# Attention with a learned position bias and a dense block: bias rows read from a gapped table, a new hand-written order, and one store per half of the last block

## The chip, the cores and the metric

The kernel runs on one core of one Trainium2 chip. The metric is the device time of one execution in microseconds; three executions of the kernel before took 640.33, 636.6 and 635.3 us, the median is 636.6. A profile is one more execution with the hardware profiler on.

The engines are named as in the profile: PE is the matrix engine (PEld its weight loads), DVE the vector engine, ACT the scalar engine, POOL the general-purpose engine (GpSimd), SP the engine whose queue issues almost all transfers here. DVE and ACT read and write both memories of the core, PSUM (where PE writes its sums) and SBUF; POOL reads and writes SBUF.

## What is computed

```
scores = q @ k^T / sqrt(64)              # 4 batches, 8 heads, 576 positions, 64 wide
x      = log1p(|i - j|) / log1p(max(i, 1))
bias   = relu(x * w1 + b1) @ w2          # hidden size 32, one column of w2 per head
attn   = softmax(scores + bias)          # with 1e-9 in the denominator
out    = attn @ v                        # heads joined: 2304 tokens of 512
h      = relu(out @ w_in)                # 512 -> 2048
result = (h * h) @ w_out                 # 2048 -> 512
```

Inputs and result are in 32 bit, the weights of the dense block arrive as 64-bit numbers. Products are made in 16 bit from a high and a low part of each operand, three matmuls for one, so everything that PE reads is split first.

## The kernel before

**Stages.** The 2304 tokens are ten blocks of 128 to 256 rows (two batches, five stretches of positions; the blocks of 64 positions take two batches into one tile, the others are 256 rows). For each of 80 pairs of block and head there are: scores on PE (qk, into one PSUM tile sc), one softmax step per batch on DVE that combines scores and bias and finds the extreme (L656, 144 in all), the exponential on ACT (L669), a conversion into high and low parts on ACT and POOL (L710, L712), a transpose (by PE for the first heads, by a DMA later), and the product with v (pv). When a block's eight heads are done it is scaled (norm) and transposed, and the dense block runs over its 16 hidden tiles in eight steps: 24 matmuls (g1, L837), a square (ACT L849, DVE L851, a cast, POOL L857), and the second product (g2, L872). The last block of 64 positions has its output halved in columns and is stored by `store` (L882 to 898).

**Before the steady state.** Two things are built in the first 240 us beside the attention. First the weights: each of 32 tiles of w_in and w_out is loaded as 64-bit numbers (`w_dma`), turned into a 32-bit number by three DVE instructions (L362 and L364 into PSUM, L369 into SBUF), and split by ACT and POOL (L278, L394). Second the bias: 36 groups of 16 positions, 4 rows of a small table each (`hgen`, tiles hg), multiplied by w2 on PE (`bias_mm`, L542), scaled by ACT or DVE (`bias_out`) and written to DRAM (biasd), from where each softmax step reads its bias tile (bt). The four groups of the first block are computed as max(table x w + c, ...) (L471, or ACT's L469). The 32 other groups use a table that was multiplied by -w1 once (ACT, L508, in place, so it must wait until the first four groups have read it) and take the minimum of it and one number per partition and row (DVE L477, 88 instructions, or ACT L473 with a relu, 40 instructions). They read L columns, 304 to 576, in one plain run.

**The order.** Nothing is scheduled by a compiler here. PROGRAM is a long text of some 2,550 words; each word names a step (hg:4.0 is half of the bias rows of the fifth group, ws:9 one piece of the ninth weight tile, sa a softmax step, bo a piece of the bias output, ou a store), and each occurrence lets that step issue its next instructions. Every engine then runs its own instructions strictly in that order and waits, through semaphores, for what an instruction needs. Transfers go through SP's queue in that order as well. A late instruction therefore holds up all that stands behind it on its engine.

**Names that the change touches.** tab_t holds the table (LW = 576 columns) and the scales; h2 is the buffer for two bias rows of S = 576 columns each; PATS and HID choose for each group how many of its four rows ACT computes (only the first three patterns are in use); hcst holds constants, its fourth column -w1; sm_t holds w1, b1 and w2.

Of the kernel before, what the change touches and what calls it, by code (L numbers as in the profile page):

```python
# [8 lines left out]
F32 = mybir.dt.float32  # L9
# [16 lines left out]
LW = 576  # L26
# [4 lines left out]
PATS = ["DDDD", "ADDD", "AADD", "DDDP", "DDPP", "ADDP", "ADPP", "AADP", "AAPP", "DPPP"]  # L31
# [170 lines left out]
def tile_attention_moe(  # L202
# [56 lines left out]
    sel = const.tile([128, 32], F32, name="sel")  # L259
    rows_s = const.tile([128, 36], F32, name="rows_s")  # L260
    nb1 = const.tile([128, 1], F32, name="nb1")
    hcst = const.tile([128, 4], F32, name="hcst")

    eps = const.tile([128, 2], F32, name="eps")
    esc = const.tile([128, 1], F32, name="esc")
# [752 lines left out]
```

## Time and profile before

| | us |
|---|---|
| median of three executions | 636.6 (635.3 to 640.33) |
| the profiled execution, its device time | 637.86 |
| its span from the first to the last instruction | 636.1 |
| PE busy | 597.7 (94%) |
| DVE busy | 428.1 (67%) |
| POOL busy | 385.4 (61%) |
| ACT busy | 366.5 (58%) |

A view of windows gives, for stretches of the span, how long each engine was busy in it; a group of instructions gives how many there are, their busy time together (overlaps counted once) and the mean length of one. Instructions of one engine overlap a little at their ends, so a group's busy time is a bit less than count times mean. A timeline row is an instruction, or a run of equal ones, with its start and length.

### The profile page before, as it was taken

The page shows a single profiled execution, that of the slowest core. Times are in us where ns is not written, and L with a number is a line of the kernel's source. Part 1 is how long each engine was busy: PE and PEld are TensorE (multiplying, and loading weights), DVE is VectorE, ACT ScalarE, POOL GpSimd, SP SyncE. Part 2 cuts the span into 40 slices and gives each one's busy share as a digit, 9 for nine tenths or more (in the row PEclk, how much of TensorE's full clock was granted, in tenths as well). Part 3 has the DMA queues.
Part 4 walks back from the last instruction along what each step waited for, and adds up shares of the span by engine and source line. Part 5 has one row for each costly group of instructions (what it writes and reads, how often), then busy time and mean ns, then how long its engine had stood idle before and what let it go on. Part 6 is the DMA issues. An engine that isn't in the chain of part 4 may idle for free.

```text
span 636.1 us, 15958 instructions
## 1 busy us (share of the span) xinstructions
PE 597.7 (94%) x6296; PEld 402.7 (63%) x6296; DVE 428.1 (67%) x840; ACT 366.5 (58%) x779; POOL 385.4 (61%) x389
## 2 busy tenths in 40 slices
PE   5658998899999999999999999999999999999997
PEld 2124576475767467667657865767676686577576
DVE  7988999899669796787974663566456463613321
ACT  5559997687777465645567455746636574214020
POOL 5766499989767435866866647555665555523221
PEclk9669999899999999999999999999999999999999
DMA  8999987778979969799789969559955787623000
GB/s 291 325 285 284 286 237 253 244 188 203 191 183 185 220 159 170 184 226 221 177 164 219 165 131 186 139 115 196 186 136 122 158 169 144 140 34 72 18 34 18
DMA packets 204426, 112.19 MB, mean 176 GB/s; under 512 B 166848, under 2 KB 179392, under 8 KB 204352
## 3 DMA queue, kind: packets, MB, share of 16 engines
q1 hardware_dynamic: 204272, 111.12, 75.2%
q8 instruction: 49, 0.80, 0.5%
q14 instruction: 25, 0.20, 0.1%
q10 hardware_dynamic: 80, 0.07, 0.0%
HBM read 55.44 MB, written 15.61 MB: 112 GB/s over the span
## 4 chain that ended last, share of the span: by engine, by line
PE 51%; DMA 5%; DVE 5%; POOL 4%; issue 3%; ACT 2%; SPq 1%; POOLq 0%; DVEq 0%; ACTq 0%
PE hp L837 20%; PE o L872 19%; PE pv L757 5%; PE sc L637 5%; DMA at<-a 3%; DMA xt<-xh 2%; POOL a L712 2%; PE bp L542 1%; DVE s L656 1%; POOL g L857 1%; DVE g L280 1%; ACT s L669 1%; DMA stg<-vd 1%; DVE r L851 1%; ACT a L276 1%
## 5 line engine op out<-in xcount | busy, mean ns | idle before, releaser
L837 PE MATMUL hp<-xt,winH 128*128 128x256 f16 (+1 forms) x1280 | 193.3, 262 | 2.0 <-DVE r L851 1.1
L872 PE MATMUL o<-woutH,g 128*128 128x512 f16 (+1 forms) x608 | 186.4, 369 | 2.2 <-POOL g L857 1.6
L837 PE MATMUL hp<-xt,winL 128*128 128x256 f16 (+1 forms) x640 | 161.7, 262 | 0.0
L857 POOL TENSOR_TENSOR g<-r,g 128x512 f16<-128x512 f32 (+1 forms) x80 | 88.4, 1108 | 88.3 <-DVE g L280 81.5
L872 PEld LDWEIGHTS <-g 128*128 128x128 f16 x912 | 84.3, 98 | 90.5 <-issue 4.5
L712 POOL TENSOR_TENSOR a<-s,a 128x1024 f16<-128x1024 f32 (+1 forms) x64 | 133.1, 2079 | 0.0
L837 PEld LDWEIGHTS <-winH 128*128 128x128 f16 x1280 | 117.8, 98 | 20.6 <-DVE r L851 1.2
L656 DVE CUSTOM_DVE_ANT_0 s<-sc,bt 128x576 f32<-128x576 f32 x144 | 104.6, 749 | 35.7 <-PE sc L637 15.2
L851 DVE TENSOR_TENSOR r<-hp,r 128x512 f32<-128x512 f32 (+1 forms) x80 | 50.7, 634 | 105.6 <-ACT r L849 105.2
L872 PE MATMUL o<-woutL,g 128*128 128x512 f16 (+1 forms) x304 | 112.1, 369 | 0.0
L669 ACT ACTIVATE s<-s,nm 128x576 f32<-128x576 f32 x120 | 92.9, 774 | 6.6 <-ACT nm L667 0.4
L710 POOL TENSOR_TENSOR a<-s,a 128x128 f16<-128x128 f32 (+1 forms) x64 | 30.3, 473 | 105.6 <-ACT a L276 73.7
L849 ACT ACTIVATE r<-hp 128x512 f32<-128x512 f32 (+1 forms) x80 | 43.7, 546 | 85.4 <-PE hp L837 75.2
L757 PE MATMUL pv<-v,at 128*128 128x64 f16 (+5 forms) x2112 | 87.8, 203 | 1.9 <-ACT at L276 1.2
L667 ACT ACTIVATE nm<-mx,esc 128x1 f32<-128x1 f32 x120 | 34.4, 287 | 84.2 <-DVE mx L656 84.0
L276 ACT ACTIVATE a<-s 128x1152 f16<-128x1152 f32 (+1 forms) x64 | 70.3, 1098 | 14.6 <-DMA at<-a 13.5
L837 PEld LDWEIGHTS <-winL 128*128 128x128 f16 x640 | 62.6, 98 | 5.8
L757 PEld LDWEIGHTS <-at 128*128 128x128 f16 (+1 forms) x1792 | 55.0, 100 | 10.4 <-issue 3.6
L477 DVE TENSOR_SCALAR hg<-tab_t 128x464 f32<-128x464 f32 (+17 forms) x88 | 60.9, 723 | 0.7 <-PE bp L542 0.6
L280 DVE TENSOR_SCALAR g<-r 128x512 f16<-128x512 f32 (+1 forms) x64 | 48.0, 754 | 18.4 <-PE o L872 17.4
L637 PE MATMUL sc<-k,q 64*128 64x128 f16 (+1 forms) x768 | 58.2, 284 | 1.3 <-DVE mx L656 1.2
L637 PEld LDWEIGHTS <-q 64*128 64x128 f16 x768 | 39.6, 94 | 28.1 <-issue 19.0
(88 smaller groups left out, 687.1 us busy)
## 6 DMA issues: line engine op xcount, KB each, us to landing
bt<-biasd SPq DMA_DIRECT2D x64, 288.0 KB, 3.5
stg<-w_in SPq DMA_DIRECT2D x16, 512.0 KB, 6.0
stg<-w_out SPq DMA_DIRECT2D x16, 512.0 KB, 5.5
biasd<-be SPq DMA_DIRECT2D x16, 295.5 KB, 6.2
bt<-biasd SPq DMA_DIRECT2D x32, 144.0 KB, 4.7
qst<-qd SPq DMA_DIRECT2D x32, 128.0 KB, 3.3
out<-o SPq DMA_DIRECT2D x16, 256.0 KB, 2.5
v<-vd SPq DMA_DIRECT2D x8, 320.0 KB, 7.0
```

The source lines that it names most:

```text
L276: nc.scalar.activation(out=out, in_=in_, func=AF.Copy, scale=scale)
L280: nc.vector.tensor_scalar(out, in_, scale, None, op0=ALU.mult)
L477: nc.vector.tensor_scalar(ht, src, scl[:, n:n + 1], None, op0=ALU.min)
L637: i = nc.tensor.matmul(out=sc[:, o:o + w], lhsT=qt[r, qz, qs], rhs=kt[r, z, k0:k0 + w], start=(m == 0), stop=(m == 2), tile_position=(64 * ...
L656: nc.vector.tensor_tensor_reduce(s[:, 576 * b:576 * b + 576], sc[:, sb:sb + 576], bt, inv, 3.0e38, ALU.add, ALU.min, mx[:, b:b + 1])
L669: nc.scalar.activation(out=sl, in_=sl, func=AF.Exp, scale=-1.0, bias=mx[:, b:b + 1] if f32 else nm[:, b:b + 1], accum_out=su[:, h, b:b + 1])
L712: eng.tensor_tensor(av[:, :, 640:1152], ev[:, :, 0:512], av[:, :, 0:512], op=ALU.subtract)
L757: nc.tensor.matmul(out=dst, lhsT=lhsT, rhs=rhs, start=b not in [x[1] for x in seq[:j]], stop=b not in [x[1] for x in seq[j + 1:]], tile_po ...
L837: nc.tensor.matmul(out=hp[:, f * T:f * T + T].rearrange("p (b t) -> p b t", b=nb), lhsT=wt[:, k, c0:c0 + 128], rhs=xt[:, 0:nb, z * 4 + k, ...
L851: nc.vector.tensor_tensor(rr, hp[:, 0:2 * T], rr, op=ALU.mult)
L857: eng.tensor_tensor(g[:, 1, 0:2 * T], rr, g[:, 0, 0:2 * T], op=ALU.subtract)
L872: nc.tensor.matmul(out=blk["o", b][:, 0:256] if halved else blk["o", b], lhsT=g[:, z, c0:c0 + 128], rhs=wt[:, 2 * u + f, d], start=(u == 0 ...
```

## The change

**The table.** The product of the table with -w1 goes into a tile of its own, rows_t, as 36 rows of 16 numbers at a distance of 17, so that there is a gap of one number behind each row. ACT writes it with the same one instruction as before. The 32 groups with the minimum read this tile. On DVE the number of rows read, m, is made odd (L // 16 with its last bit set), so up to 16 columns more are computed than before, and the result is written as one plain run of 16 m numbers. Where L is 576, m is 36 and the result is written as 36 rows of 16 too. ACT's rows read L // 16 rows and write rows of 16.

**The last block's store.** For each half of the columns the two batches' 64 rows, which were two transfers (the last one on ACT's queue), are now one, on SP's queue.

**The order.** PROGRAM is replaced as a whole; the steps are the same but for the stores.

```diff
-PATS = ["DDDD", "ADDD", "AADD", "DDDP", "DDPP", "ADDP", "ADPP", "AADP", "AAPP", "DPPP"]
+PATS = ["DDDD", "ADDD", "AADD", "AAAD", "AAAA"]
...
-    "st tb:1 qd:0 st st tb:0 st st st st st st st qd:0 qd:0 qd:0 kd:0.0 wd:0 rs sc wd:1 sc hc sc sc hg:1.0 rs "
+    "st st tb:1 qd:0 st qd:0 st qd:0 st st st st st kd:0.0 wd:0 tb:0 kd:0.1 rs wd:1 rs wd:4 ks:0.0 vd:0.0 vd:0.1 "
...
+    rows_t = const.tile([128, 37, 17], F32, name="rows_t")
...
-    hcst = const.tile([128, 4], F32, name="hcst")
+    hcst = const.tile([128, 5], F32, name="hcst")
+    nw1 = const.tile([128, 1], F32, name="nw1")
...
             hg[gi, t] = ht
+            if gi >= 4:
+                m = min(L // 16 | 1, 36)
+                ht = h2[:, (t % 2) * S:(t % 2) * S + 16 * m]
+                src = rows_t[:, 0:m, 0:16]
+                if pat(gi)[t] == "A":
+                    m, ht, src = L // 16, ht[:, 0:L], src[:, 0:L // 16]
+                ht = ht.rearrange("p (m l) -> p m l", l=16) if m % 2 == 0 or pat(gi)[t] == "A" else ht
...
             elif pat(gi)[t] == "A":
                 nc.scalar.activation(out=ht, in_=src, func=AF.Relu, bias=scl[:, n:n + 1], scale=-1.0)
-            elif pat(gi)[t] == "P":
-                nc.gpsimd.tensor_scalar(ht, src, scl[:, n:n + 1], 1.0, op0=ALU.min, op1=ALU.mult)
             else:
                 nc.vector.tensor_scalar(ht, src, scl[:, n:n + 1], None, op0=ALU.min)
...
-        nc.scalar.activation(out=tab_t[:, 0:LW], in_=tab_t[:, 0:LW], func=AF.Identity, scale=hcst[:, 3:4], bias=0.0)
+        nc.scalar.activation(out=rows_t[:, 0:36, 0:16], in_=tab_t[:, 0:LW].rearrange("p (m l) -> p m l", l=16), func=AF.Identity, scale=nw1, bias=0.0)
...
-                for bb in range(2):
-                    r0 = (2 * p + bb) * S + 512
-                    q = nc.scalar if d and bb else nc.sync
-                    q.dma_start(out=out[r0:r0 + 64, r], in_=o[64 * bb:64 * bb + 64, 0:256])
-                    if not d or not bb:
-                        yield
+                dst = out[2 * p * S + 512:2 * p * S + 576, r]
+                dst = bass.AP(tensor=dst.tensor, offset=dst.offset, ap=[[S * DM, 2]] + [list(x) for x in dst.ap])
+                nc.sync.dma_start(out=dst, in_=o[:, 0:256])
+                if not d:
+                    yield
...
-        nc.vector.tensor_scalar(hcst[:, 3:4], sm_t[:, 0:1], -1.0, None, op0=ALU.mult)
+        nc.vector.tensor_scalar(nw1, sm_t[:, 0:1], -1.0, None, op0=ALU.mult)
```

What the new order moves is shown at three places. The first is the start of SP's queue, where the first transfers of the program are issued; tab_t and sm_t are the two small tables, stg the buffers of 64-bit weights, kst and qst those of k and q. Before:

```order
L942 DMA tab_t<-tabs 128x720
L944 DMA sm_t<-sm 128x34
L416 DMA qst<-qd 64x4x64 x2
L299 DMA kst<-kd 128x576
L346 DMA stg<-w_in 128x2x256 x2
```

and in the changed kernel:

```order
L948 DMA tab_t<-tabs 128x720
L418 DMA qst<-qd 64x4x64
L301 DMA kst<-kd 128x576
L348 DMA stg<-w_in 128x2x256
L950 DMA sm_t<-sm 128x34
L301 DMA kst<-kd 128x576
```

sm_t moved from the second to the fifth place, behind one transfer each of q, k and w_in.

The second is the start of DVE, behind its four memsets; w2s, sclw and nb are scaled copies of parts of sm_t, ci is the first result of the weight conversion, rows_s a copy of scales that PE has spread. Before:

```order
L947 TENSOR_SCALAR w2s<-sm_t 128x32
L949 TENSOR_SCALAR sclw<-tab_t,sm_t 128x16
L951 TENSOR_SCALAR nb_135<-sm_t 128x1
L953 TENSOR_SCALAR hcst<-sm_t 128x1
L500 COPY rows_s<-cp 128x36
L471 TENSOR_SCALAR hg<-tab_t,sclw,nb_135 128x544
```

and in the changed kernel:

```order
L507 COPY rows_s<-cp 128x36
L364 TENSOR_SCALAR ci<-stg 128x512
L953 TENSOR_SCALAR w2s<-sm_t 128x32
L955 TENSOR_SCALAR sclw<-tab_t,sm_t 128x16
L957 TENSOR_SCALAR nb_136<-sm_t 128x1
L959 TENSOR_SCALAR nw_138<-sm_t 128x1
L366 SCALAR_TENSOR_TENSOR ci<-stg,ci 128x512
```

The first weight step now stands ahead of all that reads sm_t.

The third is DVE just ahead of the ninth square (r<-hp,r, the first that is 512 wide, of the second block of tokens); s,mx<-sc,bt is a softmax step, hg are bias rows, xh the scaled first block. Before:

```order
L656 ISA s,mx<-sc,bt 128x576
L656 ISA mx 128x1
L820 SCALAR_TENSOR_TENSOR xh<-x,cc,xh 128x512
L477 TENSOR_SCALAR hg<-tab_t 128x480 x3
L656 ISA s,mx<-sc,bt 128x576
L656 ISA mx 128x1
L771 RECIPROCAL rd<-rd 128x8
L656 ISA s,mx<-sc,bt 128x576
L656 ISA mx 128x1
L477 TENSOR_SCALAR hg<-tab_t 128x496 x3
L280 TENSOR_SCALAR q<-qst 128x512
L851 TENSOR_TENSOR r<-hp,r 128x512
```

and in the changed kernel:

```order
L364 TENSOR_SCALAR ci<-stg 128x512
L858 TENSOR_TENSOR r<-hp,r 128x256
L366 SCALAR_TENSOR_TENSOR ci<-stg,ci 128x512
L663 ISA s,mx<-sc,bt 128x576
L663 ISA mx 128x1
L663 ISA s,mx<-sc,bt 128x576
L663 ISA mx 128x1
L371 SCALAR_TENSOR_TENSOR cv<-stg,ci 128x512
L484 TENSOR_SCALAR hg<-rows_t,tab_t 128x464
L364 TENSOR_SCALAR ci<-stg 128x512
L484 TENSOR_SCALAR hg<-rows_t,tab_t 128x464
L858 TENSOR_TENSOR r<-hp,r 128x512
```

The square stands ahead of the bias rows of two groups and of four softmax steps that it followed before, and the last weight steps (L364 to L371) now stand beside it. Counted over the whole row, 50 hg of the minimum and 30 softmax steps are ahead of it in place of 57 and 34; ahead of the 32nd L371 there are nine squares, 30 softmax steps and 51 hg in place of five, 28 and 48; ahead of the first square 34 hg, 20 softmax steps and 20 first weight steps in place of 36, 19 and 21.

## Rows read from the trace of the kernel before

**Rows 1.** windows: start:end, length, each engine's busy us (x count), PE clock, DMA share, GB/s:
```profile
0.00:80.00 80.00, 55.38 (x484) 26.62 (x484) 71.20 (x142) 55.68 (x119) 49.05 (x63) 0.87 0.96 295
80.00:160.00 80.00, 73.64 (x730) 50.76 (x729) 75.75 (x147) 65.02 (x146) 74.92 (x89) 0.98 0.82 224
160.00:240.00 80.00, 79.93 (x909) 52.82 (x908) 63.85 (x132) 51.67 (x107) 48.28 (x43) 1.00 0.90 187
240.00:600.00 360.00, 357.25 (x3847) 247.93 (x3844) 210.59 (x405) 189.20 (x400) 206.34 (x188) 1.00 0.74 153
```

**Rows 2.** windows, all engines, the stretch from 100 to 150 us:
```profile
100.00:150.00 50.00, 44.61 (x457) 30.98 (x458) 45.89 (x92) 36.72 (x82) 45.95 (x58) 0.97 0.80 221
```

**Rows 3.** source line L477: duration ns min/median/max, first and last start us, commonest shapes:
```profile
L477 DVE TENSOR_SCALAR hg<-tab_t x88: 365/500/2346, 17.9 to 238.1; 128x464 f32<-128x464 f32 x7, 128x480 f32<-128x480 f32 x7, 128x496 f32<-128x496 f32 x7, 128x512 f32<-128x512 f32 x7
```

**Rows 4.** timeline: start us, length us, engine, line, operation, tiles, shapes:
```profile
60.47 0.45 DVE L477 TENSOR_SCALAR hg<-tab_t 128x448 f32<-128x448 f32 x1
63.18 1.31 DVE L477 TENSOR_SCALAR hg<-tab_t 128x448 f32<-128x448 f32 x1
63.09 1.16 POOL L394 TENSOR_TENSOR winL<-cv,winH 128x512 f16<-128x512 f32 x1
```

**Rows 5.** groups by shape, DVE: xcount | busy us, mean ns | idle before:
```profile
L851 DVE TENSOR_TENSOR r<-hp,r 128x512 f32<-128x512 f32 x64 | 44.0, 688 | 87.9 <-ACT r L849 87.5 <-DMA qst<-qd 0.2
L851 DVE TENSOR_TENSOR r<-hp,r 128x256 f32<-128x256 f32 x16 | 6.7, 419 | 17.7 <-ACT r L849 17.7
L573 DVE TENSOR_SCALAR be<-bp,rows_s,hcst 128x480 f32<-128x480 f32 x1 | 0.8, 769 | 0.0
```

**Rows 6.** source line L362:
```profile
L362 DVE TENSOR_SCALAR ci<-stg x32: 673/686/712, 15.6 to 141.0; 128x512 uint32<-128x512 uint32 x32
```

**Rows 7.** groups by line, the first 160 us:
```profile
L477 DVE TENSOR_SCALAR hg<-tab_t 128x320 f32<-128x320 f32 (+12 forms) x55 | 38.1, 716 | 0.3 <-PE bp L542 0.2
```

**Rows 8.** groups by line and shape, DVE, the first 160 us: narrowest and widest:
```profile
L477 DVE TENSOR_SCALAR hg<-tab_t 128x304 f32<-128x304 f32 x6 | 3.3, 569 | 0.3 <-PE bp L542 0.2
L477 DVE TENSOR_SCALAR hg<-tab_t 128x496 f32<-128x496 f32 x1 | 2.0, 1999 | 0.0
```

**Rows 9.** window 80 to 160 us, instructions of L477 alone: DVE busy (x count):
```profile
80.00:160.00 80.00, 19.61 (x25) 0.98 0.82 224
```

**Rows 10.** source line L857 from 80 to 160 us:
```profile
L857 POOL TENSOR_TENSOR g<-r,g x8: 672/794/990, 104.2 to 154.0; 128x256 f16<-128x256 f32 x8
```

**Rows 11.** timeline of the start, DVE and SP's queue:
```profile
4.05 0.18 DVE L947 TENSOR_SCALAR w2s<-sm_t 128x32 f32<-128x32 f32 x1 [3.04 <-DMA sm_t<-sm]
1.72 1.41 SPq L416 DMA_DIRECT2D qst<-qd  x2
3.82 0.94 SPq L346 DMA_DIRECT2D stg<-w_in  x2
```

**Rows 12.** tile stg, the first 16 us: transfers w_in:
```profile
DMA to landing us min/median/max: 4.3/5.6/6.6
```

**Rows 13.** groups by line and shape, DVE, the first 160 us: softmax step:
```profile
L656 DVE CUSTOM_DVE_ANT_0 s<-sc,bt 128x576 f32<-128x576 f32 x34 | 25.1, 746 | 3.2 <-DMA bt<-biasd 1.5 <-DMA stg<-w_out 1.4 <-PE tp L688 0.2
```

**Rows 14.** timeline, DVE, the ninth square:
```profile
162.91 0.68 DVE L851 TENSOR_TENSOR r<-hp,r 128x512 f32<-128x512 f32 x1
```

**Rows 15.** source line L369:
```profile
L369 DVE SCALAR_TENSOR_TENSOR cv<-stg,ci x32: 666/680/689, 17.3 to 143.8; 128x512 uint32<-128x512 uint32 x32
```

**Rows 16.** timeline of the end, DMA issues:
```profile
632.18 0.56 ACTq L895 DMA_DIRECT2D out<-o  x1
632.80 0.54 SPq L895 DMA_DIRECT2D out<-o  x1
```

**Rows 17.** DMA issues by line: xcount, KB each, median us to landing:
```profile
out<-o SPq DMA_DIRECT2D x3, 64.0 KB, 2.0
out<-o SPq DMA_DIRECT2D x2, 128.0 KB, 3.2
```

**Rows 18.** who waited for whom: us in total, times, longest us:
```profile
PEld bp L542 <- DVE hg L477: 13.4, 11, 4.5
```

296 rows, old and new, of the table PROGRAM are left out of this document.

## Prediction, made blind

> **What bounds the kernel now.** I read the windows by stage first [rows 1]. From 240 to 600 us TensorE (PE) is busy for 357.25 of 360 us, from 160 to 240 for 79.93 of 80: there it is the bound, and what the vector engines save there moves nothing. Before 160 us it idles for 24.6 us (0 to 80) and 6.4 us (80 to 160), while VectorE (DVE) is busy for 71.20 and 75.75 and GpSimd (POOL) for 74.92 of the second 80. So until about 160 us DVE sets the pace, from 80 us on together with POOL, and an instruction that is shortened there brings the whole PE-bound rest forward. Between 100 and 150 us PE lacks 5.4 us [rows 2].
>
> The edited line comes next [rows 3]. Its 88 instructions (hg) take 365 ns at the least and 2346 at the most, at widths that differ by less than two. The timeline shows why [rows 4]: an hg of 448 columns takes 0.45 us when POOL rests, and 1.31 us when it starts at 63.18, just after a POOL subtraction of 1.16 us has begun (63.09 to 64.25); it ends 0.24 us behind that one. So the two engines exclude each other while such an instruction runs. DVE's first weight step (L362), which reads one tensor of SBUF at one element per cycle and writes PSUM, never waits like that: 673 to 712 ns in 32 of them [rows 6]. The Trainium skill says the same (SBUF — State Buffer, Terms): DVE and GpSimd take the shared pair of ports exclusively, for a whole instruction.
>
> **The change, part by part.**
>
> (a) Bias rows with the minimum. The table is copied into 36 rows of 16 with a gap of one word, and an odd number of rows is read into one plain run, so that source and result no longer have the same shape. I expect these hg to lose the fast mode, to cost one cycle per element, and to wait for nobody. No row of before shows this form. One element costs 1.05 ns: 128x512 from PSUM takes 688 ns, 128x256 takes 419 [rows 5], so 269/256. An hg of 448 alone, at two elements per step, takes 0.45 us [rows 4], of which 448 x 0.525 = 0.235 is width and 0.21 the fixed part. A slow hg then costs 0.21 + 0.00105 n us; at 480 that is 0.71, below the 0.769 of the nearest row, a scaling from PSUM with two scalars per partition [rows 5].
>
> Until 160 us there are 55 hg with a mean of 716 ns [rows 7], 39.4 us together, in 13 widths from 304 (six) to 496 (one) [rows 8]; over the widths the mean is 385 columns, and 393 with the rows added to make the count odd. Slow they would take 55 x 0.21 + 55 x 393 x 0.00105 = 11.6 + 22.7 = 34.3 us. **DVE saves 5.0 us**, most of it from 80 us on: there 25 of them are busy for 19.61 us [rows 9] and, at a mean of 427, would take 16.5. After 160 us the hg gain nothing (33 more, three of which stay 576 wide and fast), but PE is the bound there. Bounds: with 0.06 us more each, as at the 769 ns row, the saving is 1.7; with the fixed part of the 688 ns row (0.15) it is 8.3.
>
> POOL gains in the same stage, where it is as full as DVE: its g subtractions of 256 columns take 672 ns at the least and 794 at the median there [rows 10]. So neither keeps the other from using the saving; ACT (65.02 of 80 [rows 1]) has room.
>
> A rule of the Trainium skill speaks against the gap (Vector Engine (DVE) Microarchitecture Reference, Measured stream behaviour on trn2): pairs of words that start on an odd word cost 1.30 instead of 1.054 ns per column, and with 17 words from row to row every second row starts so. By that, an estimate, the 55 would lose 2.7 us of the 5.0. The trace's nearest row speaks for no loss: L362 reads every second word and keeps its 686 ns [rows 6]. I take the row.
>
> (b) The copy in its own tile. ACT's scaling of the table moves to a new target and no longer has to wait until the first rows have read the old one. ACT is busy for 55.68 of the first 80 us [rows 1]; zero. The scalar in a tile of its own, the wider hcst and the shorter list of patterns change no instruction, since only the first three patterns are in use.
>
> (c) The new order, at its start. The small table sm_t is the second transfer now, and DVE begins with it at 4.05 us [rows 11]. In the changed kernel it is the fifth, behind a q, a k and a weight transfer, and a first weight step stands ahead of all that reads it on DVE. That weight transfer is issued at 3.82 now; with sm_t and one q behind it instead of ahead (a q issue takes 0.70, sm_t's about 0.46) it is issued at 2.7. It lands 4.3 us later at the least, 5.6 at the median [rows 12]: 7.0 us. **DVE starts 2.9 us later.** Bounds: 0, as far as the transfers (DMA share 0.96 in 0 to 80 [rows 1]) and not DVE set the pace there, and 4.2 at the median landing. I take the full 2.9, since DVE hardly waits for transfers later on: its softmax steps did for 2.9 us in 160 [rows 13].
>
> (d) The new order, further on. Counted in the order, the first square (r, DVE) has 34 hg, 20 softmax steps and 20 first weight steps ahead of it instead of 36, 19 and 21. The ninth, the first that is 512 wide and the first of the second block of tokens, has 50 hg and 30 softmax steps instead of 57 and 34; it starts at 162.91 us now [rows 14]. Seven hg at 0.70 and four steps at 0.75 [rows 13] are 7.9 us less ahead of the second block's work, beside what (a) saves on the others. With that work at hand earlier, PE can fill part of the 5.4 us that it lacks from 100 to 150 us. Which gaps it meets no row tells: between 0 and 5.4; I take about half, **2.6 us**, since the first of these gaps lie beside the first block's squares, before the second can be ready. What moves back in return are the last weight steps (rival 4).
>
> (e) One store per half. ACT issues its store at 632.18, as soon as DVE's half is there, and SP issues the last of its three at 632.80 [rows 16]; one of 64 KB lands 2.0 us after issue [rows 17], at 634.8. With two stores SP issues the second at about 632.2. One of 128 KB takes 2.0 to 3.2 us (the rows of 64 and of 128 KB [rows 17], the latter under load); I take 2.3, nearer to the idle queue: 634.5. **0.3 us** sooner, between 0.6 sooner and 0.6 later.
>
> Sum: -5.0 + 2.9 - 2.6 - 0.3 = -5.0 us. The profiled span of 636.1 becomes 631.1. That execution took 637.86 in all, 1.3 above the median of 636.6, so I put the change on the median: **631.6 us**. About 1% (6.4 us) is what a measurement of this kernel can tell from no change.
>
> **The rivals.**
> 1. *More than the sum.* The late start costs nothing, since transfers pace the start, and the second block fills all 5.4 us: -5.0 - 5.4 - 0.3 = -10.7, 626 us. For it: PE's weight loads waited 13.4 us in their fixed order for an hg [rows 18], whose length no order could foresee while POOL decided it. Against: three bounds have to fall together.
> 2. *The saving is hidden.* Before 80 us (a) saves nearly nothing (30 hg, 38.1 less 19.61 = 18.5 us busy [rows 7, 9], against 17.8 slow) and the start is late; from 80 us on POOL's or ACT's work ends last and passes on 1 of the 4 us: +2.9 - 1 - 0.3 = +1.6, 638 us. For it: POOL's 74.92 beside DVE's 75.75 [rows 1]. Against: POOL is freed as well.
> 3. *The form does not take*: the engine joins the rows as before, or excludes POOL all the same. Then (a) is 0 and the rest stands: +2.9 - 2.6 - 0.3 = 0, 636.6. Here the Trainium skill's rule is on the side of the change (the same microarchitecture page, Performance modes): a two-port mode wants an even outermost count, or equal ones. A variant is the gap that costs: one extra element per row of 16 is 55 x 24.6 x 1.05 ns = 1.4 us, 633 us.
> 4. *Slower.* The last weight step (cv, L369) comes later: the 32nd has nine squares, 30 softmax steps and 51 hg ahead of it instead of five, 28 and 48: 4 x 0.5 + 2 x 0.75 + 3 x 0.7 = 5.6 us, and 2.9 from the start. It starts at 143.8 us now [rows 15]. It carries w_out for the last hidden unit, and every block's last products wait for it in PE's fixed order. If PE has nothing else to do ahead of them, all 8.5 us show: 636.6 + 8.5 - 0.3 = 645. It decides from the point where PE reaches such a product before it is full, at about 150 us.
>
> **How the numbers follow.** The sum as forecast 0.42, with its own range from 628 to 635; rival 1 0.25; rival 2 0.14; rival 3 with its variant 0.10; rival 4 0.09. The range from 624.5 to 639 takes in the first three and most of rival 3, and leaves out rival 4 and far ends, under 0.2. Faster by over 1% (below 630.2) is most of rival 1 and a third of the forecast: 0.39. Slower by over 1% (above 643) is rival 4: 0.09. Within 1%: 0.52.
>
> **What would show it.** For (a): hg between 0.5 and 0.85 us at every width but 576, and their sum in the first 160 us near 34. For (c): DVE's first weight step near 7 us. For (d): the first square of 512 before 157 us, and PE busy for more than 47 of 100 to 150. For (e): two stores, the second issued as DVE's half ends. I am wrong if hg still show lengths over 1 us, if PE is full later than at 150 us, or if PE loses more than 3 us behind 160 us, where I counted nothing.

## The result and the profile after

| | before | changed |
|---|---|---|
| median of four executions, us | 638.08 (635.3 to 640.33) | 643.89 (641.6 to 647.28) |
| ratio, 95% interval | | 1.0118 (1.0083 to 1.0153) |
| the profiled execution: time and span, us | 637.86, 636.1 | 641.6, 639.9 |

The change costs 1.2%, between 5.3 and 9.8 us. A second comparison, with six executions of the changed kernel against 23 of the one before, gave 1.0152 (1.0113 to 1.0191). I had forecast 631.6 us, from 624.5 to 639: the time lies above the range.

The windows of the changed kernel, to be laid beside [rows 1] and [rows 2] (columns as there):

```profile
0.00:80.00 80.00, 54.55 (x520) 30.10 (x520) 69.14 (x148) 58.31 (x126) 50.65 (x65) 0.91 0.96 299
80.00:160.00 80.00, 75.13 (x782) 54.75 (x778) 73.22 (x146) 66.11 (x144) 75.67 (x91) 1.00 0.81 225
160.00:240.00 80.00, 78.38 (x896) 48.51 (x892) 65.55 (x133) 50.47 (x104) 46.36 (x43) 1.00 0.88 191
240.00:600.00 360.00, 350.25 (x3787) 244.71 (x3786) 205.25 (x398) 187.72 (x396) 201.39 (x184) 1.00 0.73 150
100.00:150.00 50.00, 47.64 (x507) 33.46 (x505) 47.20 (x92) 38.62 (x81) 47.00 (x59) 1.00 0.84 229
```

Read the matmul counts first. By 160 us PE has done 520 + 782 = 1302, against 1214 before: 88 more, although its busy time is about the same (its clock was lower before, 0.87 and 0.98 against 0.91 and 1.00). So the front did come forward. Not all 88 are the change's: e8 below, with the old order and the old rows, has 1242 by then in its own profile.

```profile
0.00:80.00 80.00, 55.36 (x499) 27.18 (x499) 72.73 (x148) 57.52 (x122) 50.94 (x65) 0.89 0.96 300
80.00:160.00 80.00, 73.47 (x743) 51.86 (x742) 77.17 (x145) 66.30 (x149) 75.91 (x89) 1.00 0.85 226
```

By 600 us only some 15 of the 88 are left (the mix of long and short matmuls differs, so this is rough): from 160 to 240 us PE is idle for 1.62 us, where it lacked 0.07, and from 240 to 600 us for 9.75 us, where it lacked 2.75. This is the stretch that I had counted as nothing, and one of my signs of being wrong was a loss of more than 3 us there.

The end is the other place. The last instructions and two windows of one microsecond, first before, then changed:

```profile
631.66 0.48 DVE L887 TENSOR_SCALAR o<-o,os 128x256 f32<-128x256 f32 x1 [3.94 <-PE o L872]
632.18 0.56 ACTq L895 DMA_DIRECT2D out<-o  x1
633.00:634.00 1.00, 0.00 (x0) 0.00 (x0) 0.00 (x0) 0.00 (x0) 0.00 (x0) 1.00 0.56 136
```

```profile
631.26 1.90 SPq L901 DMA_DIRECT2D out<-o  x2
632.09 0.48 DVE L894 TENSOR_SCALAR o<-o,os 128x256 f32<-128x256 f32 x1 [5.02 <-PE o L879]
635.00:636.00 1.00, 0.00 (x0) 0.00 (x0) 0.00 (x0) 0.00 (x0) 0.00 (x0) 0.50 0.14 49
```

I call the time from the end of DVE's last product to the end of the span the tail. DVE's last product ends at 632.57, and the span at 639.9: a tail of 7.3 us. Before it was 4.0 (632.14 to 636.1). While the two stores run, the DMA share is 0.14 (about two of sixteen engines) at 49 GB/s; before it was 0.56 at 136 GB/s. The difference of the tails, 3.4 us, is nearly the whole difference of the two spans (3.8): in these two executions the front's gain and the loss behind 240 us cancel.

### The profile page after: what moved, and what is told of

Same layout as the page of the kernel before. It is cut to its first block, busy times and chain, and to the rows that moved or that the text cites. A ratio compares the mean times of both kernels' runs of the same rounds, so it can differ in the third digit from the quotient of the medians.

```text
span 639.9 us, 15963 instructions
## 1 busy us (share of the span) xinstructions
PE 590.3 (92%) x6296; PEld 402.3 (63%) x6296; DVE 420.1 (66%) x840; ACT 367.5 (57%) x779; POOL 381.5 (60%) x389
## 4 chain that ended last, share of the span: by engine, by line
PE 46%; DMA 18%; POOL 14%; DVE 8%; issue 6%; SPq 3%; ACT 3%; DVEq 0%; POOLq 0%; ACTq 0%
PE hp L844 20%; PE o L879 15%; DMA at<-a 8%; PE pv L764 5%; PE sc L644 3%; DMA xt<-xh 3%; POOL a L719 3%; POOL g L864 2%; DMA bt<-biasd 2%; SPq L726 2%; DVE s L663 2%; PE bp L549 1%; POOL v L280 1%; PE sc L630 1%; DMA v<-vd 1%
## 5 line engine op out<-in xcount | busy, mean ns | idle before, releaser
L864 POOL TENSOR_TENSOR g<-r,g 128x512 f16<-128x512 f32 (+1 forms) x80 | 87.1, 1090 | 108.2 <-DVE g L282 98.4
L484 DVE TENSOR_SCALAR hg<-rows_t,tab_t 128x496 f32<-128x496 f32 (+9 forms) x88 | 56.0, 669 | 0.5 <-PE bp L549 0.5
L282 DVE TENSOR_SCALAR g<-r 128x512 f16<-128x512 f32 (+1 forms) x64 | 41.3, 646 | 19.1 <-PE o L879 18.4
```

The costliest lines, as they stand in the source:

```text
L484: nc.vector.tensor_scalar(ht, src, scl[:, n:n + 1], None, op0=ALU.min)
L864: eng.tensor_tensor(g[:, 1, 0:2 * T], rr, g[:, 0, 0:2 * T], op=ALU.subtract)
```

## The experiments

All times are ratios to the kernel before, executed on the same chip between them; us are the ratio times 635.5, about the median of those executions.

| run | what it is | ratio (95%) | us |
|---|---|---|---|
| e1_store | old order and rows, merged store | 1.0076 (1.0050 to 1.0103) | +4.8 |
| e2_oldstore | changed kernel, old stores | 1.0094 (1.0063 to 1.0125) | +6.0 |
| e3_rows | old order, gapped rows | 1.0014 (0.9995 to 1.0033) | +0.9 |
| e4_order | new order, old rows | 1.0224 (1.0195 to 1.0253) | +14.2 |
| e5_front | rows, new order to 235 us, then old | 0.9981 (0.9959 to 1.0003) | -1.2 |
| e6_back | rows, old order to 235 us, then new | 1.0107 (1.0078 to 1.0136) | +6.8 |
| e7_start | rows, new order to 24 us, then old | 1.0045 (1.0022 to 1.0067) | +2.9 |
| e8_plain | old order and rows, store of 128 rows | 0.9984 (0.9964 to 1.0004) | -1.0 |
| e9_moved | e2 with eight words moved | 1.0017 (0.9996 to 1.0038) | +1.1 |
| e10_mix | e5 with the old start | 0.9985 (0.9961 to 1.0009) | -1.0 |
| e11_again | the changed kernel | 1.0152 (1.0113 to 1.0191) | +9.7 |
| e12_moved2 | e9, one word placed better | 1.0025 (1.0001 to 1.0050) | +1.6 |

**The store.** e1 makes this part of the change alone:

```diff
-                for bb in range(2):
-                    r0 = (2 * p + bb) * S + 512
-                    q = nc.scalar if d and bb else nc.sync
-                    q.dma_start(out=out[r0:r0 + 64, r], in_=o[64 * bb:64 * bb + 64, 0:256])
...
+                dst = bass.AP(tensor=dst.tensor, offset=dst.offset, ap=[[S * DM, 2]] + [list(x) for x in dst.ap])
+                nc.sync.dma_start(out=dst, in_=o[:, 0:256])
```

> The kernel before with nothing but one store per half of the last block (the old order and the old bias rows). Theory A, two causes: the changed kernel's tail shows that such a store moves 48 GB/s with about a seventh of the DMA engines busy and ends 6.5 us after its issue instead of 2. So this alone costs what the tails differ by, (639.9 - 632.57) - (636.1 - 632.14) = 3.4 us: about +3.4 us on the kernel before, PE's work unchanged. Theory B, the store is harmless and the end of the changed kernel was drawn out by what ran before it (its order, the lower granted clock there): -0.3 to +0.5 us.

+4.8 us (3.2 to 6.5): theory A, and more than its 3.4. e8 asks whether the size or the shape is slow, with the same bytes to 128 neighbouring rows:

```diff
-                dst = out[2 * p * S + 512:2 * p * S + 576, r]
-                dst = bass.AP(tensor=dst.tensor, offset=dst.offset, ap=[[S * DM, 2]] + [list(x) for x in dst.ap])
+                dst = out[2 * p * S + 512 - 64:2 * p * S + 576, r]
```

> The kernel before with one store per half whose target is 128 rows one behind the other (outermost count 128) instead of twice 64 rows (outermost count 2); the last 64 rows of one sequence are therefore left out and 64 rows of another overwritten, with as many bytes in packets of the same 1 KB. If the outermost count of 2 is what kept such a store on two of the sixteen DMA engines: landing 2.0 to 2.5 us after issue, over 120 GB/s, and -0.5 to +0.3 us on the kernel before. If 128 KB in one transfer of 1 KB packets is slow by itself: +3 to +5 us, as with the merged store.

The last product and a window of the store, first e1, then e8, and e8's summary of its store line:

```profile
628.76 0.48 DVE L887 TENSOR_SCALAR o<-o,os 128x256 f32<-128x256 f32 x1 [3.94 <-PE o L872]
633.00:634.00 1.00, 0.00 (x0) 0.00 (x0) 0.00 (x0) 0.00 (x0) 0.00 (x0) 0.64 0.14 48
```

```profile
628.76 0.48 DVE L887 TENSOR_SCALAR o<-o,os 128x256 f32<-128x256 f32 x1 [3.94 <-PE o L872]
629.00:630.00 1.00, 0.00 (x0) 0.00 (x0) 0.24 (x1) 0.00 (x0) 0.00 (x0) 1.00 0.38 131
DMA to landing us min/median/max: 1.7/1.7/1.7
```

Both end DVE's last product at 629.24; the spans end at 637.6 and 632.1, and e8 as a whole is at -1.0 us (-2.3 to +0.3). The shape is shown to be the cause: with an outermost count of 2 the two stores, 256 KB together, keep about two engines busy for over six microseconds (both are under way, and the share stays at 0.14); with 128 each of them lands 1.7 us after its issue. The place in memory is not the cause, since the four old stores write the same rows and land 2.0 us after issue [rows 17]. The Trainium skill says this (DMA: Bandwidth & Descriptors, Rules for kernel authors): the number of engines that share a transfer follows the outermost count of its access patterns, and a count of c below 16 confines it to at most c. The 0.14 of sixteen agrees.

e2 takes the store out of the changed kernel (the first diff the other way round):

> The changed kernel with the four old stores of the last block; the gapped rows and the new order stay. Theory A (store 3.4 us, the rest in the new order): 3.4 us less than the changed kernel, so +2 to +3 us on the kernel before, PE with about 11 us of idle gaps behind 160 us as in the changed kernel (2.7 before). Theory B (all of it is the order): as slow as the changed kernel, +5.8 us.

+6.0 (4.0 to 7.9): by its number this is theory B, and A's +2 to +3 is missed. But both were counted from +5.8 for the changed kernel, the difference of the first medians; the ratio of that comparison gives +7.5, and e11 below gives +9.7. Against e11 the store costs 3.7 us here; against the first comparison 1.5. So e2's time does not decide between A and B. Only e1's 4.8 has an interval of its own (3.2 to 6.5). The tails do decide. DVE's last product in e2 and in e11, whose spans end at 636.9 and 642.3:

```profile
633.26 0.48 DVE L892 TENSOR_SCALAR o<-o,os 128x256 f32<-128x256 f32 x1 [5.02 <-PE o L877]
634.51 0.48 DVE L894 TENSOR_SCALAR o<-o,os 128x256 f32<-128x256 f32 x1 [5.02 <-PE o L879]
```

The tail is 3.2 us in e2 and 7.3 in both profiles of the changed kernel; it is 4.0 before and 8.4 in e1. So the merged store costs 4.2 us at the end of the new order and 4.4 at the end of the old one, and what is left of the changed kernel's loss is in what e2 keeps, the order and the rows.

> The changed kernel once more, beside the same runs of the kernel before. From the parts (new front -1, new order's second part +6 to +7, merged store +3.4 to +4.8): +8 to +11 us. If the store's drain is partly hidden here: +6 to +8 us.

+9.7, the upper expectation, with an interval that takes in the lower.

**Rows and order apart.** e3 is the changed kernel with the old PROGRAM and the old stores, e4 the kernel before with the new PROGRAM. In e4 some of the first rows read the table after it has been scaled in place, which the old order forbids, so part of its values is not those of the reference; its instructions are the same.

```diff
 PROGRAM = (
-    "st st tb:1 qd:0 st qd:0 st qd:0 st st st st st kd:0.0 wd:0 tb:0 kd:0.1 rs wd:1 rs wd:4 ks:0.0 vd:0.0 vd:0.1 "
...
+    "st tb:1 qd:0 st st tb:0 st st st st st st st qd:0 qd:0 qd:0 kd:0.0 wd:0 rs sc wd:1 sc hc sc sc hg:1.0 rs "
...
```

> The gapped rows alone: the kernel before's order and stores, and the bias rows with the minimum read at one element per cycle. Theory A (the rows bring their saving, and the new order gives it back behind 160 us): -3 to -5 us on the kernel before, with hg of 500 to 790 ns and PE full from 160 us on. Theory C (the old order cannot use the shorter hg, since what PE waits for there is POOL or a transfer): within 1 us of the kernel before. Theory D (the slow form costs more elsewhere than it saves): slower.

> The new order alone: the bias rows as before (two elements per step, in turns with POOL) and the four old stores. Theory A (the order brings part of the front's gain and loses more than that behind 160 us): +2 to +5 us on the kernel before, with PE's gaps behind 160 us at 8 us or more. Theory B' (the order is sound, and only the rows or the store cost): -2 to -4 us, PE's gaps behind 160 us below 4 us.

e4 is at +14.2 us (12.4 to 16.1), and neither theory had that. A's other sign is there: behind 160 us PE lacks 4.1 + 9.9 = 14.0 us.

```profile
160.00:240.00 80.00, 75.89 (x857) 47.18 (x857) 64.39 (x126) 52.88 (x109) 49.44 (x44) 1.00 0.85 186
240.00:600.00 360.00, 350.07 (x3735) 243.94 (x3732) 210.21 (x406) 190.42 (x402) 204.54 (x186) 1.00 0.73 153
```

e3's groups by line, the first 160 us, beside [rows 7]:

```profile
L482 DVE TENSOR_SCALAR hg<-rows_t,tab_t 128x336 f32<-128x336 f32 (+6 forms) x57 | 33.7, 618 | 0.1
```

The rows are as short as forecast (33.7 us for 57; 38.1 for 55 before), and the kernel is not faster for it: +0.9 us, with -0.3 to +2.1. That is theory C. DVE's busy time was not what ended last in the old order; which of POOL's, ACT's or PE's waits took the place I cannot name, and it stays open. Under the new order the same rows are worth 14.2 - 6.0 = 8.2 us, e4 against e2. (The two differ also in where the scaled table goes; for the scaling in place the trace of e4 shows one wait of 0.9 us.) This order has little patience with long hg. Neither order can be priced without saying which rows run in it.

**Where the order loses.** e5 and e6 splice the two orders after word 1328, where nearly the same steps have been issued (below, the joint of e5; the word st issues nothing there):

```diff
 sa:34 sq:19 sq:20 ks:1.2 sa:34 sa:34 sa:34 sq:20
-pv:31 sa:34 bl:37 sq:21 sa:34 ks:1.2 qk:35 sb:33
+st bl:37 ks:1.2 sa:34 sa:34 vd:1.0 pv:31 sq:21 g2:19
...
```

> Gapped rows, old stores, and a spliced order: the new order's first 1328 words (to about 235 us, past every bias row with the minimum), then what is left of the old order in the old one's sequence. Theory A (the new order's loss lies behind the splice, in its PE gaps of 240 to 530 us): PE full again behind 240 us, gaps above 0.3 us there below 3 us in all, and 1 to 3 us less than the kernel before. Theory E (the loss is made in the front: the late start and the waits of 150 to 240 us): +3 to +6 us on the kernel before, as with the whole new order.

> The reverse splice: gapped rows, old stores, the old order's first 1328 words, then what is left of the new one. Theory A: the gaps of the new order's second part (pv for transposed a, hp for transposed x, o for g, sc for a softmax step; near 268, 327, 394, 503 and 528 us) come back, 8 to 11 us in all, and the kernel is 5 to 8 us slower than the kernel before. Theory E: within 2 us of the kernel before.

240 to 600 us in e3, e5, e2 and e6, in this order:

```profile
240.00:600.00 360.00, 358.34 (x3859) 248.95 (x3855) 208.10 (x402) 187.03 (x396) 205.21 (x188) 1.00 0.73 151
```

```profile
240.00:600.00 360.00, 356.61 (x3824) 248.62 (x3821) 209.80 (x403) 189.03 (x400) 205.01 (x187) 1.00 0.74 152
```

```profile
240.00:600.00 360.00, 351.68 (x3796) 246.05 (x3792) 207.11 (x400) 189.44 (x400) 202.31 (x185) 1.00 0.72 152
```

```profile
240.00:600.00 360.00, 350.69 (x3812) 244.59 (x3811) 206.75 (x401) 190.74 (x400) 202.89 (x187) 1.00 0.74 152
```

With the old second part PE is full to 1.7 and 3.4 us, with the new one it lacks 8.3 and 9.3, whatever ran in front. In time e5 is at -1.2 us (-2.6 to +0.2) and e6 at +6.8 (5.0 to 8.6): the new second part costs 6.0 + 1.2 = 7.2 us behind the new front and 6.8 - 0.9 = 5.9 behind the old. Theory A is shown, E falls.

**Is it PE's fixed order?** The gaps in the changed kernel, and PE's groups there that waited most (240 to 600 us):

```profile
328.65 0.52 PE L764 MATMUL pv<-v,at 128*128 128x64 f16 x12 [1.39 <-DMA at<-a]
396.11 0.38 PE L844 MATMUL hp<-xt,winH 128*128 128x256 f16 x2 [1.78 <-DMA xt<-xh]
504.51 0.74 PE L644 MATMUL sc<-k,q 64*128 64x128 f16 x8 [1.79 <-DVE mx L663]
529.66 0.52 PE L764 MATMUL pv<-v,at 128*128 128x64 f16 x12 [1.16 <-DMA at<-a]
L764 PE MATMUL pv<-v,at 128*128 128x64 f16 (+1 forms) x1400 | 44.9, 194 | 3.8 <-DMA at<-a 3.8
L644 PE MATMUL sc<-k,q 64*128 64x448 f16 (+1 forms) x468 | 35.5, 284 | 2.0 <-DVE mx L663 2.0
```

The same groups before waited 0.1 us for pv, and the scores not at all:

```profile
L757 PE MATMUL pv<-v,at 128*128 128x64 f16 (+1 forms) x1428 | 46.4, 194 | 0.1
L637 PE MATMUL sc<-k,q 64*128 64x448 f16 (+1 forms) x480 | 36.4, 284 | 0.0
```

For two of these gaps the trace shows what was late, and each time it is a neighbour in another queue. At 396 us it is SP's order: xh is finished on DVE at 390.38, but SP has been issuing a transpose of a since 389.04, which takes 3.31 us to issue; the transpose of x goes out at 392.44:

```profile
389.64 0.74 DVE L827 SCALAR_TENSOR_TENSOR xh<-x,cc,xh 128x512 f16<-128x512 f32 x1
389.04 3.31 SPq L726 DMA_TRANSPOSE at<-a  x1
392.44 1.27 SPq L832 DMA_TRANSPOSE xt<-xh  x1
```

At 504 us it is POOL: the same DVE instruction takes 2.50 us instead of 0.74, since it starts just behind a subtraction of 2.31 us on POOL, and the softmax steps behind it on DVE are late with it:

```profile
500.25 2.31 POOL L719 TENSOR_TENSOR a<-s,a 128x1024 f16<-128x1024 f32 x1
500.61 2.50 DVE L827 SCALAR_TENSOR_TENSOR xh<-x,cc,xh 128x512 f16<-128x512 f32 x1
503.03 0.74 DVE L663 CUSTOM_DVE_ANT_0 s<-sc,bt 128x576 f32<-128x576 f32 x1
```

The instruction reads two operands from SBUF. The Trainium skill (SBUF — State Buffer, SBUF: two separate sides) names just this case: with two SBUF inputs DVE excludes, and is excluded by, a GpSimd instruction that reads SBUF. The row agrees.

e9 lets PE do other work first at seven gaps. Each word is taken from its place and put behind (or in front of) another:

```diff
-pv:34
 sa:36 qd:11 g2:23 tx:3.1 sb:36 bl:39 ks:1.4 sb:35 tx:3.1 vs:1.0 g2:21
+pv:34
...
-qk:69
 sb:67 sa:68 sa:68 pv:65 sa:69 sb:68 g2:54
+qk:69
...
-pv:70
 qk:72 g1:62
+pv:70
...
```

In the same way g2:27 goes behind pv:39, pv:43 behind qk:46 and a g2:30, g1:54 behind pv:56, and pv:51 and the second g2:39 go in front of g1:42.

> Gapped rows, old stores and the whole new order, with eight words moved by a few places so that at seven of its gaps behind 235 us PE does other work first: pv of heads 34, 43 and 70, the second product g2 of unit 27, the first g1 of the seventh block and the scores of head 69 come one to three products later; a g2 and a pv are brought in front of the sixth block's first g1. Theory A (PE's fixed order reaches these products before the transposes, POOL or DVE have finished, and other work was at hand): most of the 7.9 us of gaps goes, 3 to 6 us less than the new order with old stores, about the kernel before. Theory F (VectorE, GpSimd and SP's transposes set the pace there themselves, and the gaps only show it): the gaps turn up again at the next products, less than 2 us gained, +4 to +6 us on the kernel before.

+1.1 us, 4.9 less than e2. In this run the scores of head 69 had come to stand behind a softmax step that reads them. e12 puts that word right (`pv:65 qk:69`):

> The eight moved words once more, with the scores of head 69 put only behind the pv of head 65, ahead of that head's own softmax (in the earlier try they stood behind its first softmax step, which therefore read the scores of another head: part of the values was wrong, the work the same). Theory A: as there, within 0.4% of the kernel before, so 3 to 5 us less than the unmoved new order with old stores (+6.0). Theory F: +4 us or more on the kernel before, the earlier gain having come from the softmax step that did not wait for its scores.

+1.6 us, 4.4 less than e2: theory A by its time. Its window from 240 to 600 us:

```profile
240.00:600.00 360.00, 354.95 (x3866) 250.18 (x3864) 207.82 (x401) 188.96 (x400) 202.44 (x185) 1.00 0.72 150
```

PE lacks 5.05 us instead of 8.3 (6.5 in e9), so not most of the gaps went, as theory A also had it, but some 2 to 3 us. The long instruction on DVE is still there, and PE only meets it later:

```profile
495.74 2.49 DVE L825 SCALAR_TENSOR_TENSOR xh<-x,cc,xh 128x512 f16<-128x512 f32 x1
```

What still lacks stands at other products, so a part of theory F holds too.

**The late start.** e7 keeps of the new order only the first 204 words and goes on with the old one (its joint is shown), e10 takes e5 with the old order's first 206:

```diff
 ws:9 ws:8 bl:3 qk:1 ws:9 hg:9.0
-bl:3 hg:9.1 ws:9 tu:0.1 sa:1 ks:0.6
+st ws:9 hg:9.0 bl:3 ws:9 hg:9.1 wd:6
...
```

> Gapped rows, old stores, and only the new order's start: its first 204 words (to about 24 us: the small table behind a q, a k and a weight transfer, DVE's start 4 us late), then the old order. If the late start is on the path as I counted it, +2.9 us on the rows alone, so about +3 on the kernel before; if transfers set the pace of the start, within 1 us.

> Gapped rows, old stores; the old order's first 206 words (small table early, to about 24 us), then the new order to its word 1328 (about 235 us), then the old one. If the late start costs its 2.8 us also under the new order's middle part: 2 to 3 us less than the splice without the old start, so 3 to 4 us less than the kernel before. If the middle part already made it up: about 1 us less than the kernel before.

e7: +2.9, so 2.0 more than e3, just clear of their two intervals: under the old order the late start is on the path. e10: -1.0, no better than e5 (-1.2): under the new middle part it costs nothing that can be measured, though the two intervals leave some 2 us either way. My first expectation for e10 was wrong. No combination is shown to be faster than the kernel before: e5, e8 and e10 lie 1 us below it, each with an interval that reaches just over 1.

## Why the prediction was wrong, step by step

**(a) The rows: the form was right, the gain was not there.** The line of the changed kernel beside [rows 3], and two of its widths:

```profile
L484 DVE TENSOR_SCALAR hg<-rows_t,tab_t x88: 508/657/2100, 16.8 to 235.1; 128x496 f32<-128x496 f32 x14, 128x464 f32<-128x464 f32 x12, 128x336 f32<-128x336 f32 x11, 128x528 f32<-128x528 f32 x10
L484 DVE TENSOR_SCALAR hg<-rows_t,tab_t 128x464 f32<-128x464 f32 x12 | 7.8, 683 | 0.0
L484 DVE TENSOR_SCALAR hg<-rows_t,tab_t 128x304 f32<-128x304 f32 x6 | 2.9, 521 | 0.0
```

From 304 to 464 columns 162 ns are added, 1.01 ns per column for 1.05 forecast, and the formula gives 697 and 529 ns. So these hg take the slow form and do not wait (the 2100 is one of the three 576 wide, which kept the fast form), and neither the gap nor the odd words on which every second row begins have a price. Rival 3 and its variant fall. But the step from "DVE is busy 5 us less" to "the kernel is 5 us shorter" failed: e3 gives nothing. That is rival 2's outcome, a saving that is hidden, which I gave 0.14; that POOL or ACT hides it, as rival 2 had it, no run shows.

**(b)** cost nothing that a run shows; none isolates it. **(c) The late start** is there: DVE begins its work on the small table and the weights at 8.13 us, 4.1 later than before (7.0 and 2.9 forecast; the transfer took 5.4 us from its issue at 2.69, not the 4.3 that I had taken as the least). Its price of 2.9 us holds only under the old order, where e7 less e3 is 2.0. Under the new order, for which I had forecast it, e10 against e5 shows none: the lower bound, 0, came true.

```profile
8.13 0.69 DVE L364 TENSOR_SCALAR ci<-stg 128x512 uint32<-128x512 uint32 x1 [3.48 <-DMA stg<-w_in]
145.36 0.68 DVE L858 TENSOR_TENSOR r<-hp,r 128x512 f32<-128x512 f32 x1
```

**(d) The second block earlier** came where it was forecast: from 100 to 150 us PE lacks 2.4 us instead of 5.4 (3.8 in e11), and the first square of 512 starts at 145.36 instead of 162.91 (before 157 was forecast). What that is worth in time no run separates. (a), (c) and (d) together I had put at -4.7 us; e5, which holds all three, gives -1.2 (-2.6 to +0.2). Part of what is missing is that the new front is no longer full behind 160 us: from there to 240 us PE lacks 2.1 us in e5, where it lacked 0.07.

```profile
160.00:240.00 80.00, 77.88 (x892) 47.62 (x892) 64.50 (x131) 51.14 (x107) 47.45 (x42) 1.00 0.88 189
```

**(e) The store** is the first step that failed by itself: -0.3 forecast, +0.6 as its worst bound, 4.8 measured alone. I took the landing time from transfers of the same size [rows 17] and counted the issues, and left out the shape of the target. The size of a transfer does not tell how many engines it gets.

**Behind 160 us** is the second, and the larger: "there it is the bound, and what the vector engines save there moves nothing". That PE was full in the old order was a property of that order, not of the stage. My sum priced the new PROGRAM only up to where the front ends, although it was replaced as a whole, and put nothing against the rest. Its part behind the splice at 235 us cost 5.9 to 7.2 us. There PE's fixed order reaches products before their inputs are there; e12 gets 4.4 us back by moving eight words.

**Rival 4**, at 645 us and 0.09, came near the measured time by luck: the last L371 starts at 147.2 instead of 143.8 (8.5 us later were feared), and no product of PE waits for it.

```profile
L371 DVE SCALAR_TENSOR_TENSOR cv<-stg,ci x32: 666/679/703, 13.0 to 147.2; 128x512 uint32<-128x512 uint32 x32
```

The sum with terms that were measured away from the changed kernel itself: front -1.2 (e5), second part +5.9 (e6 less e3), store +4.8 (e1), together +9.5 us. The changed kernel was measured at +9.7 (7.2 to 12.1) and +7.5 (5.3 to 9.8): it fits, with two or three microseconds that these intervals cannot settle (with the 4.2 us of the tails for the store the sum is +8.9).

## What to carry to other kernels

An order that is replaced has to be read to its end: an engine that is full under one fixed order shows nothing of its waits under another, so look at what each of its products has to wait for, on the queues of the transfers too. Merging two transfers into one saves an issue and can take away most of the DMA engines; look at the outermost count of both sides first. And time saved on a busy engine counts only where the order lets somebody use it: the same rows were worth nothing measurable in one order and some 8 us in the other.

## What had not been expected of the hardware

- Two stores of 128 KB in rows of 1 KB each landed 1.7 us after issue with 128 rows outermost, and took over 6 us together with 2 outermost (131 against 48 GB/s in a window of one microsecond).
- A DVE instruction with two SBUF operands took 2.50 us instead of 0.74 beside a POOL subtraction; e12 has it once more, at 2.49.
- A transpose by DMA kept SP's queue for 3.31 us (of a) or 1.27 us (of x) at 389 to 394 us while it was issued, and what stood behind it in SP's order waited that long.
